# Value loads set between the q and k loads of the third pair, and a limit of 3072 packets in place of six loads

## The chip, the cores and the metric

The kernel runs on one core of one Trainium2 chip. The metric is device time in microseconds (us) of one execution of the program; lower is better. Times come from runs of the program on the chip, and the profile is one such execution taken by the hardware profiler.

## What is computed

Attention with a relative position bias over 8 batches, 8 heads, 576 positions and 64 elements to a head, followed by a maxout feed-forward layer over the 4608 resulting tokens:

```python
scores = scale * np.matmul(q, k.transpose(0, 1, 3, 2))
scores = scores + bias.transpose(2, 0, 1)[None, :, :, :]   # bias = bias_table[bucket of the distance]
scores = scores - np.max(scores, axis=-1, keepdims=True)
attn = np.exp(scores)
attn = attn / (np.sum(attn, axis=-1, keepdims=True) + 1e-09)
x = np.matmul(attn, v)                      # then heads side by side: 4608 x 512
h = np.maximum(np.maximum(x @ w1, x @ w2), x @ w3)      # w1, w2, w3: 512 x 768
out = h @ w_out                                         # w_out: 768 x 512
```

All inputs are float32 in HBM. The kernel works in bfloat16 with float32 sums; the loads convert on the way.

## The kernel before

**Work and its stages.** Heads are taken in four pairs (hp 0 to 3) within each batch (b 0 to 7), and the main loop (L1201) runs over all (b, hp) from batch 1 on. One visit makes the scores of one pair on TensorE, their exponentials on ScalarE, the products with the bias band on VectorE, and the sums with v of the visit before it on TensorE. The feed-forward layer of an earlier chunk of 512 tokens is spread over the visits as filling. From (3, 0) on (`ROWS`, L64) a visit uses the half arrays of TensorE for two heads at a time; `attend_rows` (L966) makes the sums with v, beginning with the tile `vt` and going on with `vx`.

**Tiles of one batch.** The first 512 positions of q and k go to `q_sb` and `k_sb`, those of v to `vx`. The last 64 positions ("tails") go to `qtail`, `ktail` and `vt`. Each has two buffers, for even and odd batches. q and k must be transposed before TensorE can use them: `transposes` (L714) returns five steps for a batch, one for each of the four pairs and one (`left`) for the tails, which SyncE issues as DMA transposes into `qT` and `kT` (L721 and L728). `places` (L1188 to L1190) says at which visit each step stands. For batch n from 4 on they are: first pair at (n-1, 1), tails in the same visit, second pair at (n-1, 2), third pair in the same visit, fourth pair at (n-1, 3). SyncE's queue also holds, in program order, the output stores (L569, three at a time and then one) and the transposes of finished attention tokens into `xT` (L1011).

**Loads.** All loads of q, k and v are issued by GpSimd, one behind another in program order. A load of one head of q or k (`load_pair`, L184) has 4 x 128 rows of 64 elements, each a packet: 512. A load of one block of 128 positions of v for all heads (`load_main`, L158) has 1024. The q tail has 512, a k or v tail half (`load_tail`, L178) has 256.

At visit (b, 1) the main loop (L1339 to L1347) queues, for batch b+1, v (`load_v`: four main loads, then two tails), the third pair and the fourth pair of q and k; then `begin_qk` queues, for batch b+2, the first pair, the q and k tails and the second pair. A pair is two loads of q and two of k. GpSimd runs ahead of TensorE, so these loads are issued as early as their waits allow.

**The pacing.** Each load from batch 2 on goes through `in_turn` (L150). It gives the load a dependence on the one six places before it (`DEEP` = 6, L65), so that GpSimd issues a load only when that one has landed. Loads also wait for the buffer that they overwrite: `vx` for the sums of two batches before (TensorE), `q_sb` and `k_sb` for the transposes of two batches before. A wait holds everything behind it in GpSimd's queue.

Of the kernel before, what the change touches and what calls it, by code (L numbers as in the profile page):

```python
# [39 lines left out]
def kernel(  # L40
# [12 lines left out]
    nc = tc.nc  # L53
    B, H, S, D = q.shape
    d_model, d_ff = moe_w1.shape
    NB = bias_table.shape[0]
    P = 128
# [4 lines left out]
    QM = 2 * QS  # L62
    KT = 4
    ROWS = (3, 0)  # L64
    DEEP = 6  # L65
    FCH = d_ff // P
    DCH = d_model // P
    NTOK = B * S
# [38 lines left out]
    def mm(*args, **kw):  # L107
        made = inorder(nc.tensor.matmul(*args, **kw))  # L108
        return made
# [6 lines left out]
    vx = [const.tile([P, KT, H, VW], BF16, name=f"vx{i}") for i in range(2)]  # L116
# [25 lines left out]
    def main_part(src, b):  # L142
        return src[b, :, 0 : KT * P, :].rearrange("h (t p) d -> p t h d", p=P)

    def tail_part(src, b, h0, h1, par):
        return src[b, h0 + par : h1 : 2, KT * P : S, :].rearrange("h p d -> p h d")

    in_flight, paced = [], []

    def in_turn(b, load):  # L150
        load = inorder(load)
        if b > 1:
            if len(in_flight) >= DEEP and paced:
                go_behind([load], in_flight[-DEEP])
            in_flight.append(load)
        return load

    def load_main(src, b, h0, h1, dst, t0=0, t1=KT):  # L158
        x = main_part(src, b)
        return [  # L160
            in_turn(b, nc.gpsimd.dma_start(out=dst[:, t, h0:h1, :], in_=x[:, t, h0:h1, :])) for t in range(t0, t1)  # L161
        ]

    def diag(dst, par, h0, h1):
# [2 lines left out]

    def load_q_tail(b):
        dst = qtail[b % 2][0 : S - KT * P].rearrange("p g (h d) -> p (g h) d", h=2)
        return in_turn(b, nc.gpsimd.dma_start(out=dst, in_=q[b, :, KT * P : S, :].rearrange("h p d -> p h d")))  # L170

    def k_diag(b, par, h0, h1):
        return diag(ktail[b % 2], par, h0, h1)
# [3 lines left out]

    def load_tail(src, b, h0, h1, dst):  # L178
        return [
            in_turn(b, nc.gpsimd.dma_start(out=dst(b, par, h0, h1), in_=tail_part(src, b, h0, h1, par)))  # L180
            for par in range(2)
        ]

    def load_pair(b, g):  # L184

        for src, dst in zip((q, k), batch[b]):
            for par in range(2):
                part = main_part(src, b)[:, :, 2 * g + par, :]
                in_turn(b, nc.gpsimd.dma_start(out=dst[:, g, :, par, :], in_=part))  # L189

    def load_left(b):

        load_q_tail(b)
        load_tail(k, b, 0, H, k_diag)

    def begin_qk(b):

        batch[b] = load_tiles(True)
        load_pair(b, 0)
        load_left(b)  # L200
        load_pair(b, 1)

    def go_behind(loads, behind):

        for load in loads if behind else ():
            tc.add_manual_dep(
                load.ins, behind.ins.name,
                mybir.DependencyInfo(mybir.DependencyClass.Sync, mybir.DependencyReason.DATA),
                reason="these loads go behind the transposes in line",
            )  # L210

    def load_v(b, h0, h1):
        load_main(v, b, h0, h1, vx[b % 2][:, :, :, 0:D])
        load_tail(v, b, h0, h1, v_diag)
# [33 lines left out]
    batch = [None] * B  # L248
# [32 lines left out]
    for vv in range(single, NB):  # L281
# [5 lines left out]
        out=pick[:, 0:NW], in0=pick[:, 0:NW], scalar1=pick[:, NW:], scalar2=None, op0=ALU.is_equal,  # L287
    ))
    constants(1)
    load_main(q, 0, KT, H, batch[0][0], 0, 2)  # L290
    load_tail(k, 0, 0, H, k_diag)
    load_main(q, 0, 0, H, batch[0][0], 2, KT)
    load_q_tail(0)
    load_tail(v, 0, 0, H, v_diag)
    for h in range(H):
# [64 lines left out]
    def pair(n, operands, pool, tag, w=CH):  # L360


        box = []

        def rows(swap, c0=0, c1=n):
            if not swap and c0 == 0:
                box.append(pool().tile([P, 2, CH], F32, tag=tag, name="psp"))
            made = []
            for c in range(c0, c1):
                for par in range(2):  # L370
                    i = par ^ swap
                    lhsT, rhs = operands[i](slice(64 * par, 64 * par + 64), c)
                    made.append(mm(
                        box[0][:, i, 0:w], lhsT=lhsT, rhs=rhs, start=not swap and c == 0, stop=swap and c == n - 1,
                    ))
            if swap:
                behind_rows(made[0], box[1])
            elif c1 == n:
                box.append(first_rows_end())

        return lambda: box[0][:, :, 0:w], rows

    def ffn(t0, nt, last, tiled=False):
        hT = ffnw.tile([P, FCH * CH], BF16, tag="hT", name="hT")
        per = CH // nt
        n_fb = FCH // per
        st = [{} for _ in range(n_fb)]
# [40 lines left out]
        def output(j):  # L428
# [3 lines left out]
            def columns(ps, c0, c1):  # L432
                for cf in range(FCH):
                    mm(
                        ps, lhsT=hT[:, cf * nt + j * P : cf * nt + j * P + P], rhs=wo_bf[:, cf, c0:c1],
                        start=(cf == 0), stop=(cf == FCH - 1),
                    )
# [23 lines left out]
        def plain_pair(n, operands, pool, tag, w=CH):  # L461

            ps = []

            def rows(swap, behind=()):
                if not swap:
                    ps.extend(pool().tile([P, CH], F32, tag=tag, name="psp") for _ in range(2))
                made = []
                for c in range(n):
                    for par in range(2):  # L470
                        i = par ^ swap
                        lhsT, rhs = operands[i](slice(64 * par, 64 * par + 64), c)
                        made.append(mm(
                            ps[i][:, 0:w], lhsT=lhsT, rhs=rhs, start=not swap and c == 0, stop=swap and c == n - 1,
                        ))
                for ins in behind:
                    go_behind(made[:1], ins)
                return made

            return ps, rows  # L480
# [80 lines left out]
        def columns(j, c0, c1):  # L561
            return lambda r, cf: (hT[r, cf * nt + j * P : cf * nt + j * P + P], wo_bf[r, cf, c0:c1])
# [8 lines left out]
        def halves(j):  # L571
            ps, rows = pair(FCH, [columns(j, c, c + QS) for c in (0, QS)], lambda: ps_f, "ff", QS)

            def end(parts=1):
                rows(True)

                def put():
                    osb = osb_tile()
                    dve_copy(osb[:].rearrange("p (i c) -> p i c", i=2), ps())
                    put_later(j, osb)  # L580
                return put
            return lambda: rows(False), end

        def plain_outputs():
            ps0, rows0 = plain_pair(FCH, [columns(j, 0, d_model) for j in range(2)], lambda: ps_a, "a")
            ps1, rows1 = plain_pair(FCH, [columns(2, c, c + QS) for c in (0, QS)], lambda: ps_f, "ff", QS)

            def end0(behind):
                rows0(True, behind)
                osb = osb_tile()  # L590
                act_copy(osb[:], ps0[0][:])
                put_later(0, osb)

                def put():
                    osb = osb_tile()
                    dve_copy(osb[:], ps0[1][:])
                    put_later(1, osb)
                return put

            def end1(behind):  # L600
                rows1(True, behind)

                def put():
                    osb = osb_tile()
                    for i in range(2):
                        dve_copy(osb[:, QS * i : QS * i + QS], ps1[i][:, 0:QS])
                    put_later(2, osb)
                return put
            return (lambda: rows0(False), end0, lambda: rows1(False), end1, [o[3]]), None
# [465 lines left out]
    def load_last_weights():  # L1075
        in_turn(0, nc.gpsimd.dma_start(out=wo_bf[:], in_=moe_w_out.rearrange("(c p) m -> p c m", p=P)))
# [124 lines left out]
    for b, hp in [(b, hp) for b in range(1, B) for hp in range(HP)]:  # L1201
# [136 lines left out]
            made, tail = ffn((b - 1) * CH, CH, False, [(b + (i + 2) // HP, (i + 2) % HP) >= ROWS for i in range(HP)])  # L1338
        if hp == 1 and b + 1 < B:  # L1339
            paced.append(b)  # L1340
            load_v(b + 1, 0, H)
            load_pair(b + 1, 2)
            if b == 1:
                load_last_weights()
            load_pair(b + 1, 3)
# [71 lines left out]
```

## Time and profile before

The three timed runs took 306.46, 308.65 and 310.13 us. The profiled execution has its own time.

| what | value |
|---|---|
| median of three runs | 308.65 us |
| the profiled execution, time | 308.58 us |
| the profiled execution, span of the core | 306.8 us |
| granted TensorE clock | 0.998 |
| TensorE idle, span 123 to 132 us | 0.00 of 9.00 us |
| TensorE idle, span 109 to 123 us | 0.75 of 14.00 us |
| TensorE idle, span 132 to 147 us | 0.49 of 15.00 us |
| TensorE idle, span 147 to 163 us | 0.00 of 16.00 us |
| v main loads, issue to landing | median 6.6 us (128 KB each) |
| q loads, issue to landing | median 5.6 us (64 KB each) |
| transposes kT<-ktail, issue to landing | median 7.6 us |
| transposes xT<-x_sb, issue to landing | median 5.6 us |

The page's row of DMA use and of bytes moved, in 40 equal slices of the span, each 7.7 us long:

```profile
DMA  9999999999999999999999999999233013202103
GB/s 162 181 203 194 175 141 132 118 155 133 217 138 105 137 157 187 174 136 136 193 183 168 204 156 152 158 181 186 21 62 123 20 36 86 96 0 103 36 0 137
```

The digits are the mean busy share of the 16 DMA engines in tenths; they stay at 9 through slice 28, about 215 us. What GpSimd's queue waited for, longest first (us in total, times, longest):

```profile
POOL k_sb L189 <- DMA vx<-in_v_dram: 13.6, 12, 2.6
POOL q_sb L189 <- DMA vx<-in_v_dram: 9.5, 9, 1.9
POOL k_sb L189 <- DMA q_sb<-in_q_dram: 7.9, 3, 5.4
```

How to read such lines: PE is TensorE's matmuls, PEld its weight loads, DVE VectorE, ACT ScalarE, POOL GpSimd, and SPq SyncE's queue. `k_sb L189 <- DMA vx<-in_v_dram` says that the instruction of line 189 that writes `k_sb` stood until a load of `vx` had landed. Almost all matmuls carry one line, L108, that of the helper that records them, so they are told apart by tile: `sct` holds scores against the key tail, `psp` products of the feed-forward layer, `a` sums with v. In a timeline a row has its start and length in us, the engine, the line, the operation and the tile, and in brackets the idle time just before it with what ended it.

### The profile page before, as it was taken

What the parts mean: (1) busy time and instruction counts of PE and PEld (TensorE: products, weight loads), DVE (VectorE), ACT (ScalarE), POOL (GpSimd) and SP (SyncE); (2) the same over time, 40 slices, a digit from 0 to 9 for tenths busy, and PEclk for the clock granted to TensorE, in tenths of its full rate; (3) what the DMA queues carried; (4) which work ended last, traced back from release to release, by engine and by line L of the source; (5) the groups of instructions that cost most, each with busy time, mean ns of one, the idle gap of its engine ahead of it and who ended that gap; (6) DMA issues with size and microseconds to landing.
All of it is one profiled execution on the core that took longest, in us unless ns stands there. A gap on an engine that the chain in (4) does not pass through costs nothing.

```text
span 306.8 us, 10991 instructions
## 1 busy us (share of the span) xinstructions
PE 295.8 (96%) x4745; PEld 183.8 (60%) x4745; DVE 206.8 (67%) x455; ACT 201.3 (66%) x270; POOL 142.7 (47%) x199
## 2 busy tenths in 40 slices
PE   7889999999999999999999999999999999999995
PEld 2357877765556665567566766676667654444442
DVE  7488888776767667676677677767777765453552
ACT  3999989977786677678776877777777730222211
POOL 8988677815748574975478666850000000000000
PEclk9999999999999999999999999999999999999999
DMA  9999999999999999999999999999233013202103
GB/s 162 181 203 194 175 141 132 118 155 133 217 138 105 137 157 187 174 136 136 193 183 168 204 156 152 158 181 186 21 62 123 20 36 86 96 0 103 36 0 137
DMA packets 165776, 40.51 MB, mean 132 GB/s; under 512 B 154584, under 2 KB 161248, under 8 KB 165728
## 3 DMA queue, kind: packets, MB, share of 16 engines
q0 software_dynamic: 105664, 16.66, 99.2%
q1 hardware_dynamic: 58304, 22.69, 40.7%
q8 instruction: 37, 0.61, 0.9%
q10 hardware_dynamic: 1760, 0.47, 0.7%
q14 instruction: 11, 0.09, 0.1%
HBM read 35.39 MB, written 9.45 MB: 146 GB/s over the span
## 4 chain that ended last, share of the span: by engine, by line
PE 67%; DMA 19%; POOL 8%; issue 2%; ACT 1%; SPq 1%; DVE 0%; POOLq 0%
PE psp L108 33%; PE ps L108 13%; PE a L108 9%; PE sc L108 6%; DMA vx<-in_v_dram 5%; DMA k_sb<-in_k_dram 4%; PE pso L108 4%; DMA xT<-in_k_dram 3%; DMA kT<-ktail 3%; DMA kT<-k_sb 2%; PE sct L108 2%; POOL vx L296 2%; DMA ktail<-in_k_dram 2%; POOL vx L161 1%; POOL q_sb L161 1%
## 5 line engine op out<-in xcount | busy, mean ns | idle before, releaser
L817 ACT ACTIVATE e<-sc 128x1024 bf16<-128x1024 f32 x128 | 129.0, 1026 | 30.4 <-PE sc L108 29.1
L108 PEld LDWEIGHTS <-w_bf 64*128 64x128 bf16 (+1 forms) x1112 | 75.8, 95 | 55.8 <-issue 2.3
L108 PE MATMUL psp<-xT,w_bf 64*128 64x512 bf16 x784 | 97.2, 376 | 0.4 <-PE psp L108 0.4
L797 DVE TENSOR_TENSOR e<-e,hank 128x512 bf16<-128x512 bf16 (+2 forms) x120 | 56.2, 473 | 14.4 <-ACT e L817 13.7
L108 PE MATMUL ps<-xT,w_bf 128*128 128x512 bf16 (+1 forms) x328 | 59.1, 332 | 0.0
L108 PE MATMUL sc<-qT,kT 64*128 64x256 bf16 (+1 forms) x352 | 48.6, 319 | 2.2 <-ACT e L817 0.9
L189 POOL DMA_DIRECT2D k_sb<-in_k_dram x48 | 35.9, 755 | 29.4 <-DMA vx<-in_v_dram 13.6
L108 PE MATMUL a<-vx,e 64*128 64x65 bf16 (+1 forms) x1664 | 45.1, 190 | 0.5 <-issue 0.5
L108 PEld LDWEIGHTS <-kT 64*128 64x128 bf16 (+1 forms) x712 | 29.9, 94 | 25.0 <-issue 6.6
L189 POOL DMA_DIRECT2D q_sb<-in_q_dram x48 | 36.1, 760 | 17.2 <-DMA vx<-in_v_dram 9.5
L108 PEld LDWEIGHTS <-e 64*128 64x128 bf16 (+1 forms) x1664 | 40.9, 95 | 5.0 <-issue 0.6
L108 PEld LDWEIGHTS <-hT 64*128 64x128 bf16 (+1 forms) x462 | 28.2, 95 | 18.8 <-DVE hT L541 1.6
L108 PE MATMUL psp<-wo_bf,hT 64*128 64x256 bf16 (+1 forms) x360 | 31.7, 305 | 0.0
L817 ACT ACTIVATE el<-sct 128x576 bf16<-128x576 f32 (+2 forms) x36 | 21.7, 605 | 14.9 <-PE sct L108 14.8
L411 ACT ACTIVATE m<-ps 128x512 bf16<-128x512 f32 x14 | 8.4, 597 | 34.3 <-PE ps L108 34.3
L108 PEld LDWEIGHTS <-el 64*128 64x128 bf16 (+1 forms) x676 | 26.4, 94 | 7.2 <-issue 4.6
L108 PE MATMUL a<-vt,el 64*128 64x65 bf16 (+1 forms) x260 | 29.6, 198 | 0.2 <-DVE m L501 0.2
L161 POOL DMA_DIRECT2D vx<-in_v_dram x28 | 24.6, 896 | 2.5 <-DMA q_sb<-in_q_dram 1.6
L541 DVE TENSOR_TENSOR hT<-psp,m 128x1024 bf16<-128x1024 f32 (+1 forms) x20 | 18.7, 956 | 9.2 <-PE psp L108 9.2
L108 PE MATMUL pso<-wo_bf,hT 128*128 128x512 bf16 (+2 forms) x102 | 21.7, 367 | 0.0
L420 DVE TENSOR_TENSOR m<-ps,m 128x512 bf16<-128x512 f32 x14 | 9.7, 692 | 17.0 <-PE ps L108 17.0
L527 DVE TENSOR_TENSOR m<-psp,m 128x1024 bf16<-128x1024 f32 x15 | 18.4, 1225 | 3.3 <-PE psp L108 3.2
(82 smaller groups left out, 292.8 us busy)
## 6 DMA issues: line engine op xcount, KB each, us to landing
out_dram<-osb SPq DMA_DIRECT2D x35, 256.0 KB, 5.1
vx<-in_v_dram POOLq DMA_DIRECT2D x28, 128.0 KB, 6.6
q_sb<-in_q_dram POOLq DMA_DIRECT2D x50, 64.0 KB, 5.6
k_sb<-in_k_dram POOLq DMA_DIRECT2D x48, 64.0 KB, 5.7
w_bf<-in_moe_w_dram POOLq DMA_DIRECT2D x2, 512.0 KB, 9.7
xT<-in_k_dram SPq DMA_DIRECT2D x6, 128.0 KB, 4.5
hank<-w_dr SPq DMA_DIRECT2D x2, 384.0 KB, 5.6
w_bf<-in_moe_w_dram POOLq DMA_DIRECT2D x1, 768.0 KB, 8.6
```

The costliest lines, as they stand in the source:

```text
L108: made = inorder(nc.tensor.matmul(*args, **kw))
L161: in_turn(b, nc.gpsimd.dma_start(out=dst[:, t, h0:h1, :], in_=x[:, t, h0:h1, :])) for t in range(t0, t1)
L189: in_turn(b, nc.gpsimd.dma_start(out=dst[:, g, :, par, :], in_=part))
L296: in_turn(0, nc.gpsimd.dma_start(out=vx[0][:, :, h, 0:D], in_=main_part(v, 0)[:, :, h, :]))
L411: nc.scalar.activation(out=st[fb]["m0"][:], in_=ps0, func=ACTF.Copy)
L420: inorder(nc.vector.tensor_tensor(out=m[:], in0=ps1, in1=st[fb]["m0"][:], op=ALU.max))
L527: return lambda: inorder(nc.vector.tensor_tensor(out=m[0][:], in0=ps1(), in1=m[0][:], op=ALU.max,))
L541: inorder(nc.vector.tensor_tensor(out=out_[:, i : i + n], in0=ps2()[:, i : i + n], in1=m[0][:, i : i + n], op=ALU.max,))
L797: put(nc.vector.tensor_tensor(out=e4[:, t, :, lo:hi], in0=e4[:, t, :, lo:hi], in1=hank[:, 2 * hp : 2 * hp + 2, c0:c1][:, :, ::-1], op=ALU. ...
L817: made = nc.scalar.activation(out=out_, in_=in_, func=ACTF.Exp, scale=inv_sqrt_d)
```

## The change

`in_turn` now also takes the packets of a load. For loads of batches 2 and 3 it counts loads as before. For loads of batch 4 and later it goes back through the loads in flight until their packets and its own would exceed `PACKETS` = 6 * 512 = 3072, and waits for the first that does not fit. The callers pass their packets, and `load_pair` can call a function before each of its four loads. At visits (b, 1) with b of 3 and more, the four main loads of v of batch b+1 no longer stand ahead of the third pair: one is queued before each of the pair's two q and two k loads, and the two v tails come behind the pair. The number of loads, their sizes and everything on the other engines' queues stay as they are.

```diff
+    PACKETS = 6 * QM
...
-    def in_turn(b, load):
+    def in_turn(b, load, packets=0):
+
         load = inorder(load)
         if b > 1:
-            if len(in_flight) >= DEEP and paced:
-                go_behind([load], in_flight[-DEEP])
-            in_flight.append(load)
+            n, free = 0, PACKETS - packets
+            while n < len(in_flight) and (n + 1 < DEEP if b < 4 else in_flight[-1 - n][1] <= free):
+                free -= in_flight[-1 - n][1]
+                n += 1
+            if n < len(in_flight) and paced:
+                go_behind([load], in_flight[-1 - n][0])
+            in_flight.append((load, packets))
         return load
...
-    def load_pair(b, g):
-
-        for src, dst in zip((q, k), batch[b]):
+    def load_pair(b, g, between=lambda t: None):
+
+        for j, (src, dst) in enumerate(zip((q, k), batch[b])):
             for par in range(2):
+                between(2 * j + par)
                 part = main_part(src, b)[:, :, 2 * g + par, :]
-                in_turn(b, nc.gpsimd.dma_start(out=dst[:, g, :, par, :], in_=part))
+                in_turn(b, nc.gpsimd.dma_start(out=dst[:, g, :, par, :], in_=part), KT * P)
...
         if hp == 1 and b + 1 < B:
             paced.append(b)
-            load_v(b + 1, 0, H)
-            load_pair(b + 1, 2)
+            if b < 3:
+                load_v(b + 1, 0, H)
+                load_pair(b + 1, 2)
+            else:
+                load_pair(b + 1, 2, lambda t: load_main(v, b + 1, 0, H, vx[(b + 1) % 2][:, :, :, 0:D], t, t + 1))
+                load_tail(v, b + 1, 0, H, v_diag)
             if b == 1:
                 load_last_weights()
             load_pair(b + 1, 3)
```

`load_main` passes 128 packets for each head that it loads, `load_tail` 32 for each head of its range, `load_q_tail` 512.

More of the change, by code (lines that the diff above doesn't have):

```diff
@@ L160, in load_main @@
         return [
-            in_turn(b, nc.gpsimd.dma_start(out=dst[:, t, h0:h1, :], in_=x[:, t, h0:h1, :])) for t in range(t0, t1)
+            in_turn(b, nc.gpsimd.dma_start(out=dst[:, t, h0:h1, :], in_=x[:, t, h0:h1, :]), P * (h1 - h0))
+            for t in range(t0, t1)
         ]
@@ L169, in load_q_tail @@
         dst = qtail[b % 2][0 : S - KT * P].rearrange("p g (h d) -> p (g h) d", h=2)
-        return in_turn(b, nc.gpsimd.dma_start(out=dst, in_=q[b, :, KT * P : S, :].rearrange("h p d -> p h d")))
+        return in_turn(b, nc.gpsimd.dma_start(out=dst, in_=q[b, :, KT * P : S, :].rearrange("h p d -> p h d")), 64 * H)
     def k_diag(b, par, h0, h1):
@@ L179, in load_tail @@
         return [
-            in_turn(b, nc.gpsimd.dma_start(out=dst(b, par, h0, h1), in_=tail_part(src, b, h0, h1, par)))
+            in_turn(
+                b, nc.gpsimd.dma_start(out=dst(b, par, h0, h1), in_=tail_part(src, b, h0, h1, par)), 32 * (h1 - h0)
+            )
             for par in range(2)
         ]
-    def load_pair(b, g):
-        for src, dst in zip((q, k), batch[b]):
+    def load_pair(b, g, between=lambda t: None):
+        for j, (src, dst) in enumerate(zip((q, k), batch[b])):
             for par in range(2):
+                between(2 * j + par)
                 part = main_part(src, b)[:, :, 2 * g + par, :]
-                in_turn(b, nc.gpsimd.dma_start(out=dst[:, g, :, par, :], in_=part))
+                in_turn(b, nc.gpsimd.dma_start(out=dst[:, g, :, par, :], in_=part), KT * P)
     def load_left(b):
```

## The prediction

> **What bounds the kernel now.** I read the page first, then the chain of waits from 95 to 165 us, then the list of waits of the two TensorE rows over 85 to 250 us, and last the GpSimd and TensorE timelines around the places that the chain names. The page's busy line and its line on the software DMA queue:
>
> ```profile
> PE 295.8 (96%) x4745; PEld 183.8 (60%) x4745; DVE 206.8 (67%) x455; ACT 201.3 (66%) x270; POOL 142.7 (47%) x199
> ...
> q0 software_dynamic: 105664, 16.66, 99.2%
> ...
> PE 67%; DMA 19%; POOL 8%; issue 2%; ACT 1%; SPq 1%; DVE 0%; POOLq 0%
> ```
>
> TensorE is 96% busy, and the queue that carries all q, k and v loads is in use nearly without pause as long as loads run. Two resources near their limit: which one sets the end is a question of stage. The last load is issued at about 205 us. The chain, in order of time, says where DMA last counts (columns: start, length, what):
>
> ```profile
> 111.32 1.18 SPq L569
> 112.60 0.45 SPq L569
> 113.14 1.62 SPq L728
> 114.86 7.95 DMA kT<-ktail
> 123.16 0.86 PE psp L108 x8
> ...
> 146.14 0.49 issue
> 146.63 0.57 PE a L108 x24
> ```
>
> The transpose of batch 4's key tail, issued at 114.86, took 7.95 us, and TensorE waited for it. From 123 us on the chain holds TensorE work and 0.49 us of "issue", no load at all. The waits of the matmul row and of the weight loads after 85 us confirm it:
>
> ```profile
> PE sct L108 <- DMA kT<-ktail: 0.7, 1, 0.7
> PE a L108 <- issue: 0.5, 1, 0.5
> ...
> PEld L108 <- DMA kT<-ktail: 0.9, 1, 0.9
> ```
>
> So what a better order of loads can win behind 109 us, where the first changed load stands, is a wait of 0.75 us (0.9 on the weight-load row), plus at most the stalls marked "issue". Comparing the same matmuls one batch later in the chain gives the rest: 128.38 to 160.36 is 31.98 us, 160.36 to 191.96 is 31.60, 191.96 to 223.26 is 31.30. The last is the undisturbed period; batches 4 and 5 lose 0.68 and 0.30 us against it.
>
> **The change, part by part.** *Instructions.* Each batch still issues 25 loads (4 v main, 2 v tails, 16 q and k, 3 q and k tails), with the same packets: 1024 for a v main load, 512 for a q or k load or the q tail, 256 for a k or v tail. Their GpSimd time stays 0.74 to 0.90 us each, and nothing but loads stands in that queue at this stage. TensorE, VectorE and ScalarE keep their order. Cost of the instructions: 0.
>
> *The limit.* 3072 packets are six loads of 512, so for q and k loads the new rule repeats the old one; a tail of 256 lets one more load in. It bites only around v, where six loads are 4 x 1024 + 2 x 256 = 4608 packets. Batches 2 and 3 keep the old rule and order: cost 0, nothing moved.
>
> *The order.* For batches 4 to 7 the queue changes from v v v v t t q q k k to v q v q v k v k t t. Before, for batch 4 (GpSimd timeline; start, length, what):
>
> ```profile
> 109.29 3.53 POOL L161 DMA_DIRECT2D vx<-in_v_dram  x4
> 112.76 0.69 POOL L180 DMA_DIRECT2D vt<-in_v_dram  x1
> 113.81 0.62 POOL L180 DMA_DIRECT2D vt<-in_v_dram  x1 [0.37 <-DMA k_sb<-in_k_dram]
> 115.21 0.75 POOL L189 DMA_DIRECT2D q_sb<-in_q_dram  x1 [0.78 <-DMA vx<-in_v_dram]
> 116.33 0.74 POOL L189 DMA_DIRECT2D q_sb<-in_q_dram  x1 [0.37 <-DMA vx<-in_v_dram]
> 118.76 0.74 POOL L189 DMA_DIRECT2D k_sb<-in_k_dram  x1 [1.69 <-DMA vx<-in_v_dram]
> 121.67 0.74 POOL L189 DMA_DIRECT2D k_sb<-in_k_dram  x1 [2.17 <-DMA vx<-in_v_dram]
> ```
>
> The times from issue to landing for these loads: v main, then v tails, then the first three of the pair:
>
> ```profile
> DMA to landing us min/median/max: 5.6/7.5/9.5
> DMA to landing us min/median/max: 8.4/8.6/8.8
> DMA to landing us min/median/max: 5.7/7.4/7.7
> ```
>
> I read from these: first v main lands at 109.29 + 5.6 = 114.9, the third at about 118.5, the fourth at 111.9 + 9.5 = 121.4, the tails at 122.2; q at 122.9 and 123.7, first k at 124.5, and the second k at about 126.6, since SyncE's transpose of that k, which waited for it, is issued at 126.63. That is 6656 packets. If the engines serve the same packets per us in another order (an estimate, and the step on which most rests), cumulative packets give the new landings: second q is the 3072nd packet, 118.5; the last v main the 5632nd, 123.7; second k the 6144th, 124.5; the v tails last, 126.6. So q of the third pair comes 5 us earlier, k 2 us, v main 2.3 us later, v tails 4.4 us later.
>
> *Who profits from q and k.* The transposes of the third pair on SyncE, issued at 123.77 and 126.63, could go at about 120.5 and 124.6. TensorE first uses that pair at 136.5, some 4 to 7 us after they land: worth 0. Behind them stand the fourth pair's transposes, which wait for loads that land as before, then the xT transposes: 0.
>
> *Who suffers from v.* First use of batch 4's v tails:
>
> ```profile
> 129.06 0.21 PE L108 MATMUL a<-vt,el 64*128 64x65 bf16 x2
> ```
>
> The cover was 129.06 - 122.2 = 6.9 us and becomes 2.5; with TensorE 0.6 us earlier, 1.9. If it went, every us of lateness would be a us of the end. For batch 5 the same sum (tails at about 154.8 against a use at 161.04) leaves 6 us, for 6 and 7 over 10. Cost 0, bounds 0 and +6 (rivals).
>
> *Added waits on GpSimd.* The second v main waits for a load of pair 1 (about 111.2 instead of 110.2), the fourth for the second v (about 117.6 instead of 111.9), and the loads of pair 4 start about 0.4 us later than 122.41. Queued behind them: the tails, pair 4, then the first pairs of batch b+2, whose transposes come a batch later. SyncE's use of batch 5's first pair has about 5 us of cover, so 0.4 us costs nothing.
>
> *The key-tail transposes.* They are issued at 113.14 and 114.86, with 4608 and about 3600 load packets in flight; now at most 3072. In the trace the tail transposes took 7.9 and 9.2 us there, 8.7 at 144.6, 7.3 at 172.8 and 5.7 to 6.2 at 202 to 205; the last three have some 2000 packets in flight and the same three stores of 256 KB just ahead of them. Mean 8.6 against 7.3 for some 2000 packets: 0.65 us per 1000. With 500 to 1500 fewer packets that is 0.3 to 1.0 us, I take 0.6. [...] The rows between 5.7 and 9.2 us show a dependence on something, though not cleanly on depth (8.7 at 144.6 fits badly). [...] I take the row, and keep 0 and -0.9 as ends.
>
> *The issue stalls.* 0.68 and 0.30 us in batches 4 and 5 look like TensorE's instruction supply under full DMA load. No row ties them to v loads; between 0 and -1.0, I take 0.
>
> **Sum.** Against the profiled execution of 308.58 us (span 306.8 and 1.8 around it): -0.6, so 308.0. The median of the three runs, 308.65, stands 0.07 above; 308.0 for the median as well. The runs spread from 306.46 to 310.13, about 1.8 us either way, more than this sum.
>
> **The rivals.** [...] *A larger gain, 306.9.* Depth sets the stalls of instruction supply too, and 0.75 + 0.68 + 0.30 = 1.7 us go. For: they occur only while loads run. Against: nothing in their rows names a load. *Slower, v arrives late.* A queue with fewer packets gets a smaller share of the engines beside stores and transposes. The 6656 packets take 17.3 us now (109.3 to 126.6). If the rate falls by more than about an eighth, the v tails land after 129.06 and TensorE stands at the first sums of batch 4, with nothing else to run. A rate down by a fifth lands them at about 131, +2, 310.6; down by a third (3072 for 4608 in flight) at 135.3, +6, 314.9. Against it: the seven loads issued between 121 and 127 us, about 3072 packets in flight, landed in 3.5 to 4.4 us,
>
> ```profile
> DMA to landing us min/median/max: 3.5/4.0/4.4
> ```
>
> so a queue of that depth loses no rate where stores are absent. I put its time at 312.
>
> **How the numbers follow.** Chances: the tail wait shrinks, 308.0, 0.47; no change 0.23; larger gain 0.13; v late 0.17. About 1% (3.1 us) is what a measurement of this kernel can tell from no change. Faster by over 1% (under 305.6) needs the whole larger gain and a favourable scatter: 0.07. Slower by over 1% (above 311.7) is a little over half of the v-late case and some scatter: 0.11. Within 1%: 0.82. The range from 305.7 to 310.4 holds the first three cases with their scatter and the mild end of v late; most of what is left out is v late.
>
> **What would show it.** Right: in the changed kernel no wait on the key tail above 0.3 us near 122; that transpose landing in about 7.3 us; q of the third pair transposed from about 120.5 in batch 4; a batch period that stays between 31.3 and 32.0 us; no TensorE wait on vx or vt. [...] A wait on SyncE's queue or on qT or kT of pairs 3 and 4 would be a mechanism that I have not seen.

## The result, and the profile after

The changed kernel takes 307.02 us (median of 22 runs, 306.22 to 310.15), the kernel before 308.88 us in the same series (22 runs, 306.46 to 312.73). The ratio is 0.9943, with a 95% interval from 0.9923 to 0.9964: faster by a little over half a per cent, 1.8 us. (The ratio leaves out slow executions, those over 1.5% above the fastest of their kernel, here four of the kernel before; medians take in all.) The forecast was 308.0 us.

The profiled execution took 306.96 us, 1.62 less than that of before. Its page, the lines that answer to those of before:

```profile
PE 295.5 (97%) x4745; PEld 183.7 (60%) x4745; DVE 206.3 (68%) x455; ACT 201.3 (66%) x270; POOL 143.7 (47%) x199
...
q0 software_dynamic: 105664, 16.66, 95.5%
...
PE 80%; ACT 7%; DMA 6%; DVE 3%; SPq 2%; issue 1%; DVEq 0%; ACTq 0%
```

TensorE's busy time is the same to 0.3 us; only its idle time shrank. The packets of the load queue, as many as before, took less time in sum (95.5% against 99.2%). What the matmul row waited for from 85 to 250 us is now this:

```profile
PE sct L109 <- DMA kT<-ktail: 0.6, 2, 0.3
PE a L109 <- DVE m L511: 0.2, 1, 0.2
```

The wait on the key tail near 122 us is 0.26 us and no longer 0.75 (the other of the two, 0.35 us, lies at 90 us, ahead of the first changed load). The line "PE a <- issue" of before is gone. In the chain of waits, the transpose of that tail and some feed-forward matmuls that stood in the prediction, now at:

```profile
115.26 6.87 DMA kT<-ktail
122.48 0.86 PE psp L109 x8
...
127.70 0.86 PE psp L109 x8
...
159.01 0.86 PE psp L109 x8
...
190.33 0.86 PE psp L109 x8
...
221.63 0.86 PE psp L109 x8
```

Matched with the same matmuls of before, they show where the time went:

```
stretch, us of before      gained    what stood there before
up to 97.98                 -0.43    (after waits 0.35 for a key tail here; nothing is changed yet)
97.98 to 128.38              1.11    0.58 at the stall of 108.1 (0.41 of it idle), 0.75 - 0.26 of the wait on the key tail
128.38 to 160.36             0.67    0.49 "issue" at 146.14, with what it held up
160.36 to 191.96             0.28    a stall of some 0.2 at 177.6
191.96 to 223.26             0.00
sum                          1.63
```

Two of these stalls in the timeline of before: the idle time at 108.1, and eight sums at 177.40 that take 0.53 us where the like groups beside them take 0.29:

```profile
108.53 1.04 PE L108 MATMUL psp<-xT,w_bf 64*128 64x512 bf16 x8 [0.41 <-PE psp L108]
...
177.40 0.53 PE L108 MATMUL a<-vx,el 64*128 64x65 bf16 x8
```

The batch period is 31.31, 31.32 and 31.30 us, where before had 31.98, 31.60 and 31.30. So the key tail brought about 0.5 us, and stalls that no load's landing ends brought the rest. The stall at 108.1 stood in the profile of before ahead of any changed load (109.29), and the execution after waits 0.35 us for the key tail at 90 us, also ahead of any change; both are luck of one execution. Without them the two profiles differ by 0.49 + 0.67 + 0.28 = 1.4 us.

GpSimd's loads of batch 4 in the changed kernel (start, length, what, idle time before):

```profile
105.43 0.89 POOL L167 DMA_DIRECT2D vx<-in_v_dram  x1 [0.98 <-PE psp L109]
106.31 0.76 POOL L199 DMA_DIRECT2D q_sb<-in_q_dram  x1
108.50 0.89 POOL L167 DMA_DIRECT2D vx<-in_v_dram  x1 [1.43 <-PE sc L109]
109.37 0.76 POOL L199 DMA_DIRECT2D q_sb<-in_q_dram  x1
110.25 0.89 POOL L167 DMA_DIRECT2D vx<-in_v_dram  x1
111.13 0.76 POOL L199 DMA_DIRECT2D k_sb<-in_k_dram  x1
114.66 0.89 POOL L167 DMA_DIRECT2D vx<-in_v_dram  x1 [2.76 <-PE a L109]
115.53 0.76 POOL L199 DMA_DIRECT2D k_sb<-in_k_dram  x1
116.28 1.26 POOL L188 DMA_DIRECT2D vt<-in_v_dram  x2
```

The landing times of the two v tails, and the first use of them on TensorE:

```profile
DMA to landing us min/median/max: 6.2/6.2/6.2
```

```profile
128.39 0.21 PE L109 MATMUL a<-vt,el 64*128 64x65 bf16 x2
```

The waits between the loads are the new limit at work (the releaser named there is TensorE, but the wait is for an earlier load: the fourth v load goes at 114.66, after the second has landed at 114.12). The last tail lands at 116.9 + 6.2 = 123.1, and 5.3 us are left.

### The profile page after: what moved, and what is told of

It reads as the page before. It is cut to its first block, busy times and chain, and to the rows that moved or that the text cites. A ratio compares the mean times of both kernels' runs of the same rounds, so it can differ in the third digit from the quotient of the medians.

```text
span 305.2 us, 11001 instructions
## 1 busy us (share of the span) xinstructions
PE 295.5 (97%) x4745; PEld 183.7 (60%) x4745; DVE 206.3 (68%) x455; ACT 201.3 (66%) x270; POOL 143.7 (47%) x199
## 3 DMA queue, kind: packets, MB, share of 16 engines
q0 software_dynamic: 105664, 16.66, 95.5%
q1 hardware_dynamic: 58304, 22.69, 41.6%
## 4 chain that ended last, share of the span: by engine, by line
PE 80%; ACT 7%; DMA 6%; DVE 3%; SPq 2%; issue 1%; DVEq 0%; ACTq 0%
PE psp L109 32%; PE ps L109 15%; PE a L109 12%; PE sc L109 8%; PE pso L109 6%; ACT e L827 5%; DMA kT<-ktail 5%; PE sct L109 2%; PE warm L109 1%; PE scq L109 1%; ACT el L827 1%; SPq L738 1%; SPq L731 1%; DVE e L807 1%; DMA out_dram<-osb 1%
```

## The experiments

Two theories stood against each other at first. A: what counts is how many load packets are in flight, because these hold up the packets that carry TensorE's instructions and SyncE's transposes. B: what counts is where the v loads stand in the order. Two more asked whether the key tail is all of the gain, and what it takes to make v late. Ratios are to the kernel before, run in the same series on the same chip; medians are only compared within a series. Of each edit the lines that matter are shown, "..." marks a cut. The median of before was 310.11 us for the first four kernels, 309.33 for the next four, 310.49 for the last four.

**The limit alone.** The order of before, with 3072 packets from batch 4 on.

```diff
-            if b < 3:
+            if b < B:
                 load_v(b + 1, 0, H)
                 load_pair(b + 1, 2)
```

> The packet limit alone; v loads stand ahead of the third pair as in the kernel before. Theory A (depth: fewer load packets in flight let TensorE's instruction blocks and the key-tail transpose land sooner): most of the gain, a ratio of 0.994 to 0.997, no stall over 0.3 us at the matmuls where the kernel before stalls with no releaser, key-tail wait near 122 us below 0.5 us. Rival B (order: what counts is where the v loads stand): ratio 0.998 to 1.002, stalls as before. Rival C (v late): a TensorE wait on vt or vx, ratio above 1.003.

Measured: 306.95 us, ratio 0.9907 (0.9872 to 0.9942). The matmul row waits for nothing from 85 to 250 us but this, which all kernels have:

```profile
PE a L109 <- DVE m L511: 0.2, 1, 0.2
```

All of the gain is here; the ratio is below the 0.994 to 0.997 that A expected.

**The order alone.** Six loads in flight whatever their packets.

```diff
-            while n < len(in_flight) and (n + 1 < DEEP if b < 4 else in_flight[-1 - n][1] <= free):
+            while n < len(in_flight) and (n + 1 < DEEP):
```

> The order alone, with six loads in flight whatever their packets: up to 3 x 1024 + 3 x 512 = 4608 packets, as deep as before. Theory A (depth): ratio 0.998 to 1.002, stalls on instruction blocks still there in the profile. Rival B (order): most of the gain, 0.994 to 0.997.

Measured: 309.03 us, ratio 0.9979 (0.9945 to 1.0013): no gain that can be told from none. Its matmul row:

```profile
PE a L109 <- issue: 1.4, 2, 1.0
```

The stalls without a releaser are still there, 0.98 and 0.39 us. The interval alone would leave room for the 0.9945 to 0.997 of B; B falls because the limit alone has all of the gain in the old order. The wait on the key tail is missing here too, with as many packets in flight as before: the transpose took longer (8.42 us), but it was issued at 110.83 and not at 114.86. So that wait also hangs on when SyncE gets to the transpose, which varies from execution to execution.

**A limit of 2048 packets.** The change, with less in flight.

```diff
-    PACKETS = 6 * QM
+    PACKETS = 4 * QM
```

> The whole change with a limit of 2048 packets in place of 3072. Theory A (depth): instruction blocks land at least as early as with 3072; as those stalls are gone already, only the key-tail wait (0.26 us with 3072) is left to win: ratio to the kernel before 0.992 to 0.995, provided that the loads keep their pace. Rival C (a smaller queue loses its share of the DMA engines): loads of batches 5 to 7 slip, the last load is issued later than 206 us by 5 us or more, TensorE waits on vt, vx, qT or kT, ratio above 1.0.

Measured: 326.34 us, ratio 1.0465 (1.0398 to 1.0531). The expectation of A failed and C came in. GpSimd's loads of batch 4, what the matmul row waited for from 100 to 260 us, and one stage of it (PE busy, then the other engines, and after POOL the granted clock of TensorE, the DMA share and GB/s):

```profile
114.00 0.89 POOL L167 DMA_DIRECT2D vx<-in_v_dram  x1 [2.93 <-PE sc L109]
...
120.02 0.88 POOL L167 DMA_DIRECT2D vx<-in_v_dram  x1 [4.39 <-PE sc L109]
...
126.07 0.88 POOL L167 DMA_DIRECT2D vx<-in_v_dram  x1 [4.41 <-DMA vx<-in_v_dram]
```

```profile
PE a L109 <- DMA vt<-in_v_dram: 11.1, 4, 4.5
PE psp L109 <- DMA xT<-x_sb: 2.7, 1, 2.7
PE sct L109 <- DMA kT<-ktail: 1.2, 1, 1.2
```

```profile
132.00:163.00 31.00, 28.31 (x551) 18.02 (x550) 17.32 (x34) 18.85 (x22) 13.40 (x18) 0.90 1.51 140
```

A v load of 1024 and a q load of 512 leave 512, so the next v load waits until the one before has landed. They go 4.6 to 6.1 us apart, one landing time (4.0 to 5.5 us) and 0.5 us more each: 16.6 us from the first (109.44) to the fourth, where 3072 took 9.2 (105.43 to 114.66). TensorE waits for v in each of the four batches. The granted clock falls to 0.90 in this stage, and 40 sums with v take 1.10 us there (at 132.38) where the same 40 take 0.62 with the change (at 129.53). That adds to the loss: the waits sum to 15 us, the profiled span is 23 us longer than that of the change (328.4 against 305.2). This execution was the longest of six (322.02 to 330.2); the granted clock was 0.97 to 0.99 in all of them.

**The transposes of the tails ahead of the stores.** The kernel before, loads untouched.

```diff
-        store_outputs()
+        if b < 3:
+            store_outputs()
         turn_ahead(b, hp, 1)
+        store_outputs()
```

> The kernel before, with SyncE's transposes of the second half of a visit (the key tails among them) put ahead of the three output stores from batch 3 on; loads untouched. If the wait on the key tail was all that the change won, this alone gives a ratio of 0.994 to 0.996. Theory A: only the 0.75 us wait goes (key tail landed at about 120, no wait near 122), the stalls on instruction blocks stay: 0.9975, between 0.996 and 0.999.

Measured: 309.18 us, ratio 0.9957 (0.9916 to 0.9999). By ratio alone it could be nothing or most of the gain; by the medians of one series it stands 0.9 us below the kernel before and 2.2 us above the limit alone. What the matmul row of the profiled execution waited for from 85 to 250 us:

```profile
PE a L108 <- DVE m L501: 0.2, 1, 0.2
```

There is no wait on the key tail. But there is no stall over 0.14 us behind 100 us either, although the loads were untouched and A expected the stalls to stay. This execution, 306.84 us, was the second shortest of twelve (306.81 to 313.74). So the stalls come and go from one execution to the next, and this run does not show how much of the gain is the tail's.

**More in flight.** The order of before, with a limit of 6144 packets: up to eight loads and 5632 packets around v.

```diff
-    PACKETS = 6 * QM
+    PACKETS = 12 * QM
...
-            if b < 3:
+            if b < B:
                 load_v(b + 1, 0, H)
                 load_pair(b + 1, 2)
```

> The old order, with the limit raised to 6144 packets from batch 4 on, which leaves eight loads in flight (up to 5632 packets around v). Theory A (depth delays TensorE's instruction blocks and the tail transposes): slower than the kernel before, ratio 1.002 to 1.012; more or longer stalls with no releaser, every one of them at a TensorE instruction whose number, counted from the first, is 193 modulo 256; key-tail wait near 122 us above 0.75 us. Rival D (3072 wins for another reason, depth beyond 4608 does nothing): ratio 0.998 to 1.002.

Measured: 320.18 us, ratio 1.0306 (1.0207 to 1.0405), a loss more than twice the upper end expected. What the matmul row waited for from 100 to 225 us, its longest stall, and a stage:

```profile
PE a L109 <- issue: 6.1, 6, 1.9
PE psp L109 <- issue: 4.1, 3, 3.2
PE psp L109 <- PE psp L109: 0.8, 1, 0.8
```

```profile
143.77 0.72 PE L109 MATMUL psp<-wo_bf,hT 64*128 64x256 bf16 x10
147.73 0.28 PE L109 MATMUL psp<-wo_bf,hT 64*128 64x256 bf16 x2 [3.24 <-issue]
```

```profile
132.00:163.00 31.00, 26.74 (x536) 17.16 (x533) 17.24 (x34) 18.61 (x22) 17.09 (x24) 0.94 1.96 160
```

TensorE stops for 3.24 us between the tenth and the eleventh of twelve like matmuls, with all operands there. Of the expectation one point missed: there was no wait on the key tail near 122 us, since the transpose was issued earlier, at 112.25, and had landed at 120.9.

**The same, 32 TensorE instructions further.** Sixteen narrow matmuls more at the start.

```diff
     on_zeros(warm[:, 0:CH], 9)
+    for _ in range(16):
+        mm(warm[:, 0:8], lhsT=zeros[:, 0:P], rhs=zeros[:, 0:8])
...
```

> The same with 16 narrow matmuls (32 TensorE instructions with their weight loads) more at the start, while TensorE waits for the first keys; their sums are not used. Theory A: the stalls with no releaser keep to instruction numbers of 193 modulo 256 in this kernel's own count, so they stand at other matmuls, those of 161 modulo 256 in the unshifted count. Rival E (the stall belongs to a place in the program, such as the sums with v): they stay at the same matmuls, 225 modulo 256 in this kernel's count. Time: the start up to 1 us longer.

Measured, in one execution: 315.46 us, with four such stalls. The longest:

```profile
138.91 0.24 PE L109 MATMUL a<-vx,el 64*128 64x65 bf16 x4
142.82 0.29 PE L109 MATMUL a<-vx,el 64*128 64x65 bf16 x4 [3.67 <-issue]
```

Numbering TensorE's instructions (matmuls, weight loads and its 49 instructions that wait or drain) from 0 in order of start gives this for the kernels with stalls, for stalls over 0.3 us behind 100 us:

```
kernel              instruction before which TensorE stood          modulo 256
before              3265, 4801                                      193
e2_order            3777, 7105                                      193
e5_deep             3265, 3521, 3777, 4033, 4289, 4545, 5057,
                    5825, 7105                                      193
e6_deep_shift       4289, 4545, 5825, 6081 (its own count)          193
f4_limit_tail_first 3265                                            193
```

(The traces of the order alone and of the last kernel, whose run is told of below, lack nine matmuls that the trace of before has, four of them ahead of these stalls; the four are counted in.) With 32 instructions put in at the start, number 4545 is another matmul, a sum with v and not a product of the feed-forward layer, and the stall is there. The place in the program doesn't matter, the place in the stream of instructions does. E falls.

**Change and tail first together.**

> The changed kernel with SyncE's second-half transposes ahead of the three output stores from batch 3 on. Theory A: the remaining key-tail wait of 0.26 us near 122 goes and nothing else: 0.999 of the changed kernel, ratio to the kernel before 0.990 to 0.994. If stores put behind transposes hold up the output buffers, VectorE waits on osb and the ratio is above 0.995.

Measured: 307.23 us, ratio 0.9965 (0.9929 to 1.0001). The profile shows no wait on the key tail, but the ratio is above the 0.990 to 0.994 expected, and the time is not below the changed kernel's by anything that these runs can tell. VectorE's waits at `osb` are as with the change (5.8 and 5.7 us in total), so the later stores held nothing up there.

**The limit for batches 2 and 3 too.** Old order, no exception for early batches.

```diff
-            while n < len(in_flight) and (n + 1 < DEEP if b < 4 else in_flight[-1 - n][1] <= free):
+            while n < len(in_flight) and in_flight[-1 - n][1] <= free:
...
-            if b < 3:
+            if b < B:
                 load_v(b + 1, 0, H)
                 load_pair(b + 1, 2)
```

> The packet limit alone, in the old order, for batches 2 and 3 too. Theory A: the stall near 108 us and the key-tail wait near 90 us, which come up in some executions, shrink as well: up to 0.7 us, ratio 0.989 to 0.993. Rival C (v late): batches 2 and 3 have less cover, TensorE or VectorE waits on v of batch 2 or 3 and the ratio is above that of the limit from batch 4 on (0.991).

Measured: 307.77 us, ratio 0.9993 (0.9963 to 1.0022): by the ratio no gain that can be told from none. By the medians of the series it stands 1.6 us below the kernel before and 0.5 us above the change with the tails first. So A's 0.989 to 0.993 did not come in, and how much of the gain is lost stays open. No stall of the kind above, but two waits for loads that came late:

```profile
PE sc L109 <- DMA kT<-k_sb: 0.9, 1, 0.9
...
PE pso L109 <- DMA wo_bf<-in_moe_w_out_dram: 0.7, 1, 0.7
```

Late were a weight that is queued behind v and the keys of a pair, not v itself as C had it.

**Four kernels side by side.** The changed kernel and the limit alone again, the change with 2560 packets, and the limit with the tails first.

> The changed kernel as it is, beside the limit alone on the same chip. Theory A (depth alone): ratio to the kernel before 0.990 to 0.997, and its median within 0.3 us of the limit alone. Rival B (order adds something): 0.6 us or more below the limit alone.

> The limit alone once more, for the comparison on one chip. Theory A: within 0.3 us of the changed kernel. Rival B: 0.6 us or more above it.

> The whole change with a limit of 2560 packets, between 2048 (late v) and 3072. With this limit a v main load, one more and a load of 512 fit together, so the queue holds two v loads at a time and not one. Theory A with rival C as its lower edge: the loads keep pace only in part; v tails of batch 4 land 1 to 3 us after they did with 3072, which had about 5 us left, so the time stays within 0.5% of the changed kernel. If the queue's rate falls as it did at 2048, TensorE waits on vt and the ratio to the kernel before is above 1.01.

> The limit alone with the tail transposes ahead of the stores. Theory A: the last TensorE waits behind 100 us are gone, time equal to the limit alone or up to 0.3 us below it, ratio to the kernel before 0.989 to 0.996.

Measured: 307.26 us, ratio 0.9940 (0.9902 to 0.9979); 307.59 us, 0.9907 (0.9875 to 0.9939); 307.79 us, 0.9911 (0.9873 to 0.9950); 307.14 us, 0.9925 (0.9889 to 0.9961). The four can't be told apart. So the new order adds nothing that shows, which is theory A. The executions of the four lie between 305.98 and 309.55 us, those of the kernel before between 306.78 and 315.27: with the limit the long executions are missing. With 2560 packets the loads fall behind: the last one is issued at 215.3 us, with 3072 at 209.6, and with the limit alone at 204.0; none of it reaches TensorE. No version beats the changed kernel by more than the scatter. Not tried was a smaller number of loads in place of six; and as each packet of these loads has 128 bytes in the traces of the kernels before and after (a q load of 512 is 64 KB), packets and bytes are not told apart.

## Why the prediction was right, and where it was not

**The time:** 307.02 us lies in the range, but 0.6 us were forecast as gain and 1.9 measured. The range held no change and the larger gain as well, so that the time lies in it does not show the mechanism.

**What bounds the kernel:** right. From 109 us on TensorE set the time (in the kernel before 22.25 us busy of 23 up to 132 us, 114.45 of 115 from there to 247), and only its waits could be won.

**The limit bites only around v, the order does nothing for q and k:** right. The limit alone gives 0.9907 twice, the order alone 0.9979 with 1 in its interval. Earlier q and k of the third pair (transposed from 120.31, forecast 120.5) were worth nothing.

**The key-tail transposes:** the size was about right, 0.49 us for 0.6. The 0.6 was read from rows of the trace, and the runs bear it out. No run shows the other end kept for this term, 0, by which the length of the software queue would not matter to the transpose and on which the chance of no change rested; in its place the runs showed this. From issue to landing, the four transposes of key tails took 7.9, 8.7, 7.3 and 6.2 us before (mean 7.6), 6.9, 5.5, 6.4 and 6.7 with the change (6.4), and 4.4, 4.6, 4.9 and 5.4 with 2560 packets (4.8). Batch 4's alone, where v is queued around it: 7.95 to 8.6 us in four kernels with 4608 packets and more (the kernel before, the order alone and the two with a limit of 6144), 6.2 to 7.9 in five with 3072, 4.4 with 2560, 5.5 with 2048. So the transpose gets shorter as the software queue does, though not in every row. The size of the gain is in part luck, since with the order alone the same wait was absent at 8.42 us.

**The issue stalls:** the step that failed. It named them as TensorE's instruction supply under full DMA load, bounded them between 0 and -1.0, and took 0 since no row tied them to v loads. They went: 0.67 and 0.28 us in these profiles, the larger part of the 1.4 us. No "issue" stall and periods of 31.3 throughout, as the larger gain would have it, is what the profile shows. The tie was to be found in the number of packets in flight: with eight loads the same stalls come to some 11 us, with a limit of 3072 packets the profiles of seven executions hold one, of 0.41 us at 108.5, ahead of that kernel's first v load (108.84). Three profiles with 4608 hold 0.9, 1.4 and, in the execution with the tails first, no such stall over 0.14, so one profile alone does not prove the tie; the lead of the instruction packets, in the last section, shows it in all three. The forecast of the rival "larger gain", 306.9 us, is nearer the 307.02 measured than 308.0, and its reason, that depth sets the stalls of instruction supply too, is the one that the runs support.

**v late:** the mechanism is real and its place was right (the first sums with `vt`), its edge was put too near. The cover in batch 4 is 5.3 us and not 2.5, since GpSimd reached the first v load at 105.43 and not at 109.29. Over the other kernels with at least 3072 packets in flight that load goes between 100.9 and 108.8 us: its start varies from execution to execution, and the one profiled before was the latest of them. At 2048 packets the case came in with 1.0465, not because the single load took longer to land (v loads of batch 4 took 3.2 to 5.5 us, with the change 4.3 to 6.8) but because the limit lets a v load go only after the landing of the one before. A smaller share of the engines for a queue with fewer packets shows on the two pages as 95.5% for 99.2%, with q1, the next in size, at 41.6% for 40.7%; no wait on v came of it.

## What to carry to other kernels

Loads that nobody waits for can still cost time. Here, with up to 4608 packets of them in flight and not 3072, the transposes of key tails took 7.6 us and not 6.4, instruction packets were through 2.29 us ahead of TensorE and not 3.08 (means, the last section has the reading), and the time was 308.88 us and not 307.02. Where loads differ in size, limit them by packets rather than by a number such as six, with just enough in flight to keep pace (here 2560 to 3072; 2048 was too few, 4608 too many), and find both edges by trying. A wait marked "issue", with operands ready, is worth counting in instructions before it is set to nothing.

## What the runs showed of the hardware

The page of the kernel after has a queue of instruction packets (packets, MB, share of 16 engines):

```profile
q8 instruction: 37, 0.61, 0.8%
```

In the trace these are 37 packets of 16 KB, and TensorE has 9,539 instructions, 258 to a packet. No view says whose instructions a packet holds; the stalls, always at one number modulo 256, are why this queue is read here as TensorE's. Every stall of over 0.3 us without a releaser behind 100 us stood before an instruction that is 193 modulo 256. From the end of the packet in question in the trace to the first matmul after the stall:

```
kernel           packet ends, us    TensorE goes on, us    between
before                    107.00                 108.53       1.5
before                    145.23                 146.63       1.4
before                    176.27                 177.70       1.4
e5_deep                   146.38                 147.73       1.4
e6_deep_shift             141.27                 142.82       1.6
```

So in these stalls TensorE goes on 1.4 to 1.6 us after the packet's end. Over the packets issued from 100 to 215 us, the lead of a packet's end over the instruction 193 modulo 256 that is read here as needing it (in these two traces the next such one) was 2.29 us on average before and never below 1.40, with the change 3.08 and never below 1.70. In the same way, for the other kernels:

```
packets in flight, at most     kernels                              mean lead, us
5632                           the two with a limit of 6144         2.06, 2.45
4608                           order alone; tails first             2.40, 2.59
3072                           the other six with this limit        2.98 to 3.54
2560                           the limit of 2560                    3.75
2048                           the limit of 2048                    5.02 (TensorE waits for v)
```

That these packets come later with more loads in flight is what the means show, 3.75 us of lead with 2560 packets down to 2.06 with 5632; where they are held up was not tried.

A second thing: in two runs with long stalls and waits of TensorE the granted clock is lower beside them. Over 132 to 163 us it was 0.94 with eight loads in flight and 0.90 with 2048 packets, and 1.00 in the kernel before and after. With 2048 packets a wait of 2.19 us for `vt` ends at 130.43 us, and just behind it the clock is at half (PE busy, the other engines, granted clock, DMA share, GB/s):

```profile
131.20:134.60 3.40, 3.40 (x82) 2.40 (x76) 1.03 (x3) 1.02 (x1) 2.13 (x3) 0.50 1.46 118
```
